# The last nine groups' q and k by rows and DMA transposes in a kernel of chunked attention and a leaky two-layer network

## The chip, the cores and the metric

The kernel runs on one core of a Trainium2 chip. The time is the device's, in microseconds, of one execution; a kernel's time is the median of its runs. The engines are TensorE (PE, with its weight loads PEld), VectorE (DVE), ScalarE (ACT), GpSimd (POOL) and SyncE (SP, which only issues DMAs here). Each engine works off its own instructions in order and waits on semaphores for the others.

## The reference

Inputs are q, k and v of 8 batches, 8 heads, 576 rows and 64 columns, and two weight matrices, all in float32.

```python
q_c = q.reshape(B, H, nc, 64, D)                       # nc = 9 chunks of 64 rows; k_c, v_c alike
scores = scale * np.matmul(q_c, k_c.transpose(0, 1, 2, 4, 3))
scores = scores - np.max(scores, axis=-1, keepdims=True)
attn = np.exp(scores)
attn = attn / (np.sum(attn, axis=-1, keepdims=True) + 1e-09)
out = np.matmul(attn, v_c)                             # attention inside each chunk alone
x = out.transpose(0, 2, 1, 3).reshape(B * S, H * D)    # 4608 tokens of 512
h = x @ w_in                                           # 512 x 2048
g = np.maximum(0.01 * h, h)
return g @ w_out                                       # 2048 x 512, float32
```

## The kernel before

**Attention, 36 groups.** A group u is 128 tokens (two chunks) of all 8 heads. Per group: q goes into a tile QZ (one of three), where each head's q stands transposed beside zeros, so that one matmul does two heads; k goes transposed into KT. Stage s multiplies them into the PSUM bank Sp (8 matmuls, L827). Stage m takes the row maximum on DVE. Then there are two forms: groups in UB (and all before UX = 14) subtract the maximum on DVE (stage b) and take one exponential of 512 columns on ACT (stage x); the others turn the maximum into a bias (stage nb) and take eight exponentials of 64 columns that also give the row sums (stage f). Stage z sums and inverts on DVE, stage n multiplies on POOL (tile en), stage d transposes en by a DMA on SP's queue into et (L916), stage v multiplies by V (L927), and stage a copies the result on ACT into xT, the transposed tokens.

**How q and k come in.** Groups before UD = 14 load their natural rows (load_qk, tiles q_in and k_in, 128 tokens on 128 partitions, cast to 16 bits) by DMAs on POOL's queue, and PE transposes them into PSUM. Groups from 14 on use load_qk_batch: per batch 16 DMAs on POOL's queue (L114) bring q and k in 32 x 32 pieces into the tiles q_d and k_d, and DVE's 32 x 32 transposes finish the work: stage dq writes QZ in two halves of 64 partitions (L804), stage dk writes KT (L814). A group that lies across two batches does each in two pieces. A batch has four and a half groups; batches 3 to 7 come in this way.

**The network, 19 blocks.** Blocks of 128 or 256 tokens follow as soon as their tokens are there. The first layer of a block is mm1 (L347, result hT, leaky unit on ACT at L361) up to block 13; from block 14 on it is done with seven products in place of eight (`wide`, L444, banks xbank and xpr, sums xs and WS of the inputs, kept parts xkeep, leaky unit at L462 on ACT or for the parts in LEAK_DVE at L458 on DVE). The second layer of nearly all blocks is also done with seven products (`product`, L245), from four sums SG of parts of the activations gT (`token_sums`, L221, on DVE) and four sums of weights; `combine` puts the products together (L288 to L309) and the result is stored from SP's queue (L321).

**The order.** PE's work is a list `chunks`, one chunk being some 8 to 16 matmuls. Everything else is an event with a due time in steps; a step is one chunk (half a step for a part of `wide`). A loop issues all events that are due, then the next chunk. The scores of group u are due at T[u], which adds up the distances in SPACE; the other stages of the group are due at fixed distances from T[u] (O_Q for dq and dk, O_Z for z, n and d, O_V and VO for v and a). `later` makes an event some steps after the present chunk, and the dict MOVED shifts single events by name, such as `'dq 32 1': -3.25`. `flush` issues pending events at once where a chunk needs them. So the emitted order on each engine's queue is set by these numbers, and the time by when each queue's head may go.

Of the kernel before, what the change touches and what calls it, by code (L numbers as in the profile page):

```python
# [8 lines left out]
FP16 = mybir.dt.float16  # L9
# [7 lines left out]
def kernel(  # L17
# [22 lines left out]
    NIN = 5  # L40
    PAIRED = range(1, 4)
    UD = 14
    LEAD = 5
    UE = 5
    UX = 14
    UB = (14, 17, 18, 19, 21, 24, 26, 27, 28, 30, 32, 34)
    G = 2 * CH

    NU = n_tok // G
# [159 lines left out]
    def token_sums(j, n):  # L209
        nh = BLOCKS[j] // 2  # L210
        one, two = rows(j)
        a11, a12 = gT[j][:, :HF, one], gT[j][:, HF:, one]
        a21, a22 = gT[j][:, :HF, two], gT[j][:, HF:, two]
        SG[j, n] = sbp.tile([128, HF, nh], FP16, name="SG", tag="gS", bufs=4, padded_shape=[128, HF, 128])
        x, y, op = {
            1: (a21, a22, ALU.add),
            2: (SG.get((j, 1)), a11, ALU.subtract),
            3: (a11, a21, ALU.subtract),
            4: (a12, SG.get((j, 2)), ALU.subtract),
        }[n]  # L220
        nc.vector.tensor_tensor(out=SG[j, n], in0=x, in1=y, op=op)  # L221

    def product(j, n, i):
        one, two = rows(j)
# [584 lines left out]
    def stage_dk(u):  # L809
        KT[u] = sbp.tile([128, 4, 2, CH], FP16, name="KT", tag="KT", bufs=3)  # L810
        for b, at, e0, n in cuts(u):
            for i in range(1, 16, 2):
                need("D", b, i)
            nc.vector.transpose(  # L814
                out=KT[u][:, :, e0:e0 + n, :],
                in_=flat(qkd[b][1])[:, :, at:at + n * CH].rearrange("p h (e t) -> p h e t", e=n),
            )
# [103 lines left out]
    def stage_v(u):  # L921
        et = ET.pop(u)
        xp = psp.tile([128, NT, 2, CH], FP32, name="xp", tag="ox", bufs=1)
        for e in range(2):
            b, c = divmod(2 * u + e, NCH)
            for t in range(NT):
                nc.tensor.matmul(  # L927
                    out=xp[:, t, e, :],
                    lhsT=VB[b % NVB][:, t, c, :],
                    rhs=et[:, t // 2, e, t % 2, :] if u < UD else et[:, t % 2, e, t // 2, :],  # L930
                    start=True,
                    stop=True,
                )
            if c == NCH - 1 and b + NVB < B:
                load_v(b + NVB)
# [48 lines left out]
    def zero_act(i):  # L984
# [162 lines left out]
```

## Time and profile before

| | |
|---|---|
| median of 3 runs | 282.65 us (282.22 to 283.72) |
| profiled execution | 283.47 us, span 281.6 us, granted clock 0.998 |
| PE busy | 271.5 us, 96% of the span |
| PEld busy | 242.1 us, 86% |
| DVE busy | 237.5 us, 84% |
| ACT busy | 189.9 us, 67% |
| POOL busy | 152.5 us, 54% |
| chain that ended last | PE 77%, DVE 9%, DMA 5%, ACT 4% |

A profile row of a group of instructions reads: line, engine, operation, out<-in by tile names, shapes, count, then busy us and mean ns of one, then idle time before them and what ended it. A row of the waits reads: who waited, for whom, us in all, times, longest. A row of the timeline reads: start, duration, engine, line, what, count, and in brackets the idle time before it. A row of stretches gives each engine's busy us and count, the granted clock, the DMA share and GB/s.

### The profile page before, as it was taken

How to read it: one execution, taken by the hardware profiler on the slowest of the kernel's cores; microseconds unless marked ns; L12 is line 12 of the kernel's file. 1: busy time of each engine (PE TensorE's matmuls, PEld its weight loads, DVE VectorE, ACT ScalarE, POOL GpSimd, SP SyncE). 2: the span in 40 equal slices, each digit the busy share in tenths (PEclk: the TensorE clock that was granted, in tenths of full speed). 3: DMA queues.
4: the chain of work that ended last, by engine and by line, in shares of the span. 5: the costliest groups of instructions: out<-in, count | busy, mean ns of one | idle time of the engine just before them, and what ended most of it. 6: DMA issues, size and time to landing. Idle time of an engine off the chain costs nothing.

```text
span 281.6 us, 8496 instructions
## 1 busy us (share of the span) xinstructions
PE 271.5 (96%) x3464; PEld 242.1 (86%) x3464; DVE 237.5 (84%) x471; ACT 189.9 (67%) x485; POOL 152.5 (54%) x182
## 2 busy tenths in 40 slices
PE   7889999999999999999999999999899999999995
PEld 4569958999998888999999999999789898999994
DVE  5876599899887978999978787999999999887674
ACT  6766734675757587657778676567568888786761
POOL 8838636878296687797569828934024151600000
PEclk9999999999999999999999999999999999999999
DMA  9999999999999999999999999999451213110213
GB/s 144 152 190 177 207 175 155 151 120 114 64 100 177 82 60 151 134 165 81 178 81 129 123 249 159 206 100 128 33 95 22 94 21 95 21 74 4 75 40 112
DMA packets 182790, 32.66 MB, mean 116 GB/s; under 512 B 173792, under 2 KB 178272, under 8 KB 182752
## 3 DMA queue, kind: packets, MB, share of 16 engines
q0 software_dynamic: 158880, 18.23, 129.7%
q1 hardware_dynamic: 22832, 13.64, 22.2%
q8 instruction: 27, 0.44, 0.7%
q10 hardware_dynamic: 1040, 0.26, 0.4%
q14 instruction: 11, 0.09, 0.1%
HBM read 36.96 MB, written 9.44 MB: 165 GB/s over the span
## 4 chain that ended last, share of the span: by engine, by line
PE 77%; DVE 9%; DMA 5%; ACT 4%; POOL 2%; issue 2%; DVEq 0%; ACTq 0%; POOLq 0%
PE hT L347 29%; PE prX L245 17%; PE prZ L245 6%; PE pr L245 6%; PE xbank L444 4%; PE xpr L444 3%; DMA VB<-in_v_dram 3%; ACT ex L858 3%; PE prW L245 2%; PE oP L489 2%; DMA k_in<-in_k_dram 2%; PE Sp L827 2%; PE xp L927 2%; DVE xkeep L480 2%; DVE QZ L804 1%
## 5 line engine op out<-in xcount | busy, mean ns | idle before, releaser
L347 PE MATMUL hT<-xT,w_inT 128*128 128x256 f16 (+1 forms) x1088 | 102.9, 248 | 0.6 <-DMA w_inT<-in_moe_w_in_dram 0.6
L347 PEld LDWEIGHTS <-w_inT 128*128 128x128 f16 x1088 | 84.1, 98 | 7.3 <-issue 0.8
L361 ACT ACTIVATE gT<-hT 128x512 f16<-128x512 f32 x104 | 61.8, 606 | 25.7 <-PE hT L347 25.5
L893 POOL TENSOR_TENSOR en<-ex,zi 128x512 f16<-128x512 f16 x26 | 28.6, 1098 | 64.3 <-DVE zi L887 15.3
L245 PEld LDWEIGHTS <-SG 128*128 128x128 f16 x544 | 51.4, 98 | 6.3 <-DVE SG L221 0.7
L245 PEld LDWEIGHTS <-gT 128*128 128x128 f16 x400 | 37.3, 98 | 4.9 <-ACT gT L462 0.8
L114 POOL DMA_DIRECT2D q_d<-in_q_dram x40 | 33.2, 832 | 5.9 <-DVE QZ L804 5.1
L245 PE MATMUL prX<-TW,SG 128*128 128x256 f16 x272 | 35.3, 273 | 0.6 <-DVE SG L221 0.6
L114 POOL DMA_DIRECT2D k_d<-in_k_dram x40 | 32.7, 817 | 1.8 <-DVE KT L814 1.1
L836 DVE TENSOR_REDUCE mx<-Sp 128x8 f32<-128x512 f32 x36 | 24.4, 678 | 9.6 <-PE Sp L827 9.4
L288 ACT ACTIVATE keep<-prX 128x256 f32<-128x256 f32 x51 | 20.1, 394 | 16.8 <-PE prX L245 16.8
L804 DVE STREAM_TRANSPOSE QZ<-q_d 64x512 f16<-64x512 f16 (+1 forms) x48 | 30.9, 650 | 0.6
L858 ACT ACTIVATE ex<-Sp,nb 128x64 f16<-128x64 f32 x80 | 24.0, 331 | 5.3 <-DVE nb L850 5.2
L480 DVE TENSOR_TENSOR xkeep<-xpr,xkeep 128x512 f32<-128x512 f32 x30 | 19.9, 679 | 6.7 <-PE xpr L444 4.4
L941 ACT ACTIVATE xT<-xp 128x512 f16<-128x512 f32 x36 | 21.9, 607 | 5.2 <-PE xp L927 5.2
L221 DVE TENSOR_TENSOR SG<-gT 128x1024 f16<-128x1024 f16 x34 | 23.7, 697 | 1.3 <-ACT gT L361 1.3
L444 PEld LDWEIGHTS <-WS 128*128 128x128 f16 x320 | 19.4, 98 | 1.3 <-issue 0.8
L462 ACT ACTIVATE gT<-xkeep 128x512 f16<-128x512 f32 x25 | 15.6, 632 | 6.7 <-DVE xkeep L480 6.7
L883 DVE TENSOR_REDUCE z<-ex 128x8 f32<-128x512 f16 x26 | 17.5, 672 | 2.7 <-ACT ex L873 2.4
L121 POOL DMA_DIRECT2D VB<-in_v_dram x16 | 18.6, 1169 | 0.4 <-PE xp L927 0.4
L473 ACT ACTIVATE xkeep<-xbank 128x512 f32<-128x512 f32 x30 | 16.7, 600 | 2.3 <-PE xbank L444 2.3
L245 PE MATMUL prX<-w_outT,gT 128*128 128x256 f16 x136 | 17.9, 273 | 0.3 <-ACT gT L462 0.3
(96 smaller groups left out, 470.9 us busy)
## 6 DMA issues: line engine op xcount, KB each, us to landing
out_dram<-osb SPq DMA_DIRECT2D x35, 256.0 KB, 4.4
VB<-in_v_dram POOLq DMA_DIRECT2D x16, 288.0 KB, 7.3
q_d<-in_q_dram POOLq DMA_DIRECT2D x40, 72.0 KB, 5.2
k_d<-in_k_dram POOLq DMA_DIRECT2D x40, 72.0 KB, 5.2
w_inT<-in_moe_w_in_dram POOLq DMA_DIRECT2D x8, 256.0 KB, 7.7
w_outT<-in_moe_w_out_dram POOLq DMA_DIRECT2D x4, 512.0 KB, 11.1
q_in<-in_q_dram POOLq DMA_DIRECT2D x11, 128.0 KB, 8.2
k_in<-in_k_dram POOLq DMA_DIRECT2D x11, 128.0 KB, 7.7
```

What stands on the lines that cost most here:

```text
L114: nc.gpsimd.dma_start(out=t[p0:p0 + 32, m, :, :, :].rearrange("p h b d -> p (h b) d"), in_=src[b, h0:h0 + 2, :, dh * 32:dh * 32 + 32].rear ...
L221: nc.vector.tensor_tensor(out=SG[j, n], in0=x, in1=y, op=op)
L245: nc.tensor.matmul(out=to[:, i, :], lhsT=left[:, f, i * 128:(i + 1) * 128], rhs=right[:, f, :], start=(j, where) not in opened, stop=(f == ...
L347: nc.tensor.matmul(out=hT[:, i, :], lhsT=w_inT[:, t, fc * 128:(fc + 1) * 128], rhs=xT[:, t, r0:r0 + tb], start=(t == 0), stop=(t == NT - 1),)
L361: nc.scalar.activation(out=gT[j][:, nf * a:nf * a + nf, c0:c0 + tb], in_=HT.pop((j, a, p)), func=AFT.Prelu, bias=0.0, scale=1.0, alpha=0.01,)
L444: nc.tensor.matmul(out=to[:, i, :], lhsT=left[:, t, i * 128:(i + 1) * 128], rhs=right[:, t], start=(n in (1, 2, 5) and t == 0 and i == 0), ...
L480: nc.vector.tensor_tensor(out=to, in0=of, in1=to, op=ALU.add)
L804: nc.vector.transpose(out=qz[s * CH:(s + 1) * CH, :, e0:e0 + n, s, :], in_=flat(qkd[b][0])[s * CH:(s + 1) * CH, :, at:at + n * CH].rearran ...
L836: nc.vector.tensor_reduce(out=MX[u], in_=SP[u], axis=AXL.X, op=ALU.max)
L858: nc.scalar.activation(out=E[u][:, i, :], in_=SP[u][:, i, :], func=AFT.Exp, bias=NB[u][:, i:i + 1], scale=SCL, accum_out=Z[u][:, i:i + 1],)
L893: (nc.gpsimd if u >= UP else nc.vector).tensor_tensor(out=E[u], in0=ex, in1=ZI.pop(u).unsqueeze(2).to_broadcast((128, 8, CH)), op=ALU.mult)
L941: nc.scalar.activation(out=xT[:, :, at:at + G], in_=xp, func=AFT.Copy, bias=0.0, scale=1.0)
```

## The change

Groups from UM = 27 on (batches 6 and 7) load natural rows again (load_qk, event g, 12 steps ahead of the transposes). SP's queue then issues two DMA transposes of 128 x 512 each: tdk straight into KT, tdq into a new tile QT, which shares the buffers of q_in. DVE copies the two halves of QT into QZ (stage cq). Stages dq and dk and the batch loads are left for groups 14 to 26 and batches 3 to 5. For these groups the heads stand in natural order again, so stage v takes et as it does before group 14.

Beside this, groups 15 and 25 join UB and group 21 leaves it; the sums 1 and 4 of block 14 move from DVE to POOL (SG_POOL); one part of block 17 moves in the leaky unit from DVE to ACT (LEAK_DVE); five distances in SPACE and nine in VO change, and the events from block 10 on (and the attention stages beside them) get other shifts in MOVED.

```diff
+    UM = 27
-    UB = (14, 17, 18, 19, 21, 24, 26, 27, 28, 30, 32, 34)
+    UB = (14, 15, 17, 18, 19, 24, 25, 26, 27, 28, 30, 32, 34)
...
-        nc.vector.tensor_tensor(out=SG[j, n], in0=x, in1=y, op=op)
+        (nc.gpsimd if (j, n) in SG_POOL else nc.vector).tensor_tensor(out=SG[j, n], in0=x, in1=y, op=op)
...
+    MOVED = {... 'tdq 33': 0.75, 'tdk 33': 1.25, 'cq 32 0': 1.5, 'cq 32 1': 3.5, 'cq 33 0': 2.0, 'cq 34 0': 2.0, 'tdk 34': 2.0, ...}
+    SG_POOL = ((14, 1), (14, 4))
-    LEAK_DVE = ((15, 1, 1, 0), (16, 0, 0, 0), (16, 0, 1, 0), (17, 1, 0, 0), (17, 1, 1, 1))
+    LEAK_DVE = ((15, 1, 1, 0), (16, 0, 0, 0), (16, 0, 1, 0), (17, 1, 0, 0))
-    S_LATER = (0, 1.5, 4, 10.5)
+    S_LATER = (0, 1.5, 4, 12.0)
-    X_LATER = (0.5, 1, 2.5, 4.0)
+    X_LATER = (0.5, 2.5, 2.5, 3.5)
-    D_T = 2.5
+    D_T = 3.0
...
+    def stage_tdk(u):
+        KT[u] = sbp.tile([128, 4, 2, CH], FP16, name="KT", tag="KT", bufs=3)
+        nc.sync.dma_start_transpose(
+            out=KT[u].rearrange("p i e c -> p i (e c)"), in_=qk[u][1].rearrange("p h d -> p (h d)")
+        )
+
+    def stage_tdq(u):
+        QT[u] = sbp.tile([128, 4, 2, CH], FP16, name="QT", tag="q_in", bufs=NIN)
+        nc.sync.dma_start_transpose(
+            out=QT[u].rearrange("p i e c -> p i (e c)"), in_=qk[u][0].rearrange("p h d -> p (h d)")
+        )
+
+    def stage_cq(u, s):
+        made.add(("dq", u, s))
+        part = slice(s * CH, (s + 1) * CH)
+        nc.vector.tensor_copy(out=QZ[u % NQZ][part, :, :, s, :], in_=QT[u][part])
...
-                    rhs=et[:, t // 2, e, t % 2, :] if u < UD else et[:, t % 2, e, t // 2, :],
+                    rhs=et[:, t // 2, e, t % 2, :] if u < UD or u >= UM else et[:, t % 2, e, t // 2, :],
...
+    O_A = 12.0
+    O_B = 15.0
+    O_C = 4.0
...
-        if u >= UD:
+        if u >= UM:
+            at(t - O_A - O_B, "g", u)
+            at(t - O_B, "tdk", u)
+            at(t - O_B + O_R, "tdq", u)
+            at(t - O_C, "cq", u, 0)
+            at(t - O_C, "cq", u, 1)
+        elif u >= UD:
...
-    for b in range(3, B):
+    for b in range(3, -(-UM * G // S)):
```

More of the change, by code (lines that the diff above doesn't have):

```diff
@@ L713, in fill @@
                 later(D_O, "O", j, a)
-    MOVED = {'xs 14 3': 0.5, 'xs 18 1': -2.25, 'xs 16 3': 0.25, 'G 13 6 0': 0.75, 'lp 18 1 0 0': -1.25, 'sum 13 3': -0.25, 'sum 15 4': -2.25, 'lx 16 1 6': -6.75, 'lp 17 1 1 0': 4.0, 'dq 32 1': -3.25, 'combX 13 1': -1.25, 'lp 14 0 0 0': -2.25, 'lp 14 1 0 0': 0.75, 'd 27': 2.25, 'dq 28 0': -5.75, 'sum 13 4': -2.25, 'a 31': 3.0, 'b 34': 1.0, 'lp 14 1 1 1': 0.5, 'lp 14 0 1 1': 2.25, 'lx 15 0 4': 1.0, 'lp 15 1 1 1': 3.5, 'WS 1': -2.5, 'lx 16 0 1': 1.25, 'lx 16 1 7': -1.5, 'sum 13 2': -1.0, 'xs 14 1': -1.25, 'lp 16 0 0 0': 1.0, 'dq 29 1': -2.0, 'combZ 12 3': -6.0, 'lx 14 0 6': 5.75, 'lx 18 1 4': -1.0, 'combW 11 2': 2.25, 'lx 15 0 1': -1.75, 'lx 14 1 1': -2.5, 'WS 4': 3.0, 'f 31 0 4': -0.5, 'lx 16 0 7': -2.25, 'combW 13 2': -0.75, 'lx 16 0 4': -2.75, 'lx 14 1 6': 1.5, 'combX 17 7': -0.75, 'z 35': -0.75, 'sum 15 3': 0.25, 'sum 13 1': -0.25, 'dq 33 0': -1.75, 'a 29': 2.0, 'combW 14 2': -1.0, 'xs 15 1': -2.5, 'combZ 10 3': -0.75, 'z 31': -0.75, 'dq 31 1': 1.75, 'z 30': -0.25, 'xs 16 2': 6.5, 's 30': -1.25, 'm 30': -0.75, 'combZ 13 5': 1.25, 'lx 14 1 7': -1.25, 'xs 14 4': 6.5, 'sum 14 4': 3.5, 'f 29 0 4': -1.25, 'WS 2': -0.25, 'WS 3': 4.25, 'G 13 7 0': 1.75, 'sum 14 1': -0.75, 'xs 15 4': -2.25, 'G 13 3 0': 3.0, 'a 28': 1.0, 'combX 14 6': 1.25, 'lp 15 0 1 1': -0.25, 'dq 31 0': -2.5, 'z 29': -1.5, 'lx 15 0 7': -3.0, 'G 13 1 0': -2.0, 'v 29': -0.5, 'x 34': -0.75, 'combX 13 7': 0.25, 'xs 17 1': 0.25, 'la 17 0 2': 6.0, 'dq 32 0': -0.5, 's 34': -0.5, 'lx 15 1 7': -0.5, 'combZ 14 5': 1.5, 'sum 14 3': -0.75, 'm 34': 0.5, 'dq 35 0': 3.75, 'combX 14 7': 0.25, 'xs 16 1': 0.75, 'd 30': 2.25, 'combX 11 4': 0.25, 'la 15 1 5': 0.5, 'lx 15 1 6': 0.25, 'v 31': -2.25, 'dk 33': -0.5, 'sum 12 1': -2.75, 'G 13 0 0': -1.75, 'xs 16 4': -1.75, 'dq 35 1': -2.75, 'f 27 0 4': -0.25, 'combZ 17 2': 0.5, 'lp 15 0 0 0': -1.25, 'd 31': 4.0, 'G 12 3 0': -1.25, 'combX 12 1': -1.0, 'dq 34 0': -2.25, 'lp 16 0 1 1': -1.75, 'D 7 12': 1.5, 'z 32': -0.75, 'n 29': -1.0, 'sum 17 4': 0.5, 'combX 18 7': -0.75, 'combW 12 2': -1.75, 'dq 29 0': -0.5, 'b 32': 2.0, 'v 26': -0.75, 'G 12 5 0': -2.75, 'sum 11 4': -0.75, 'sum 16 4': -2.75, 'lx 17 1 1': -0.5, 'combX 16 7': 3.75, 'sum 17 2': 0.25, 'lp 14 1 1 0': -3.0, 'xs 18 3': 1.5, 'lx 18 1 7': -2.0, 'combZ 15 3': 3.0, 'd 35': 1.0, 'dq 33 1': 2.0, 'v 33': -0.75, 'sum 11 2': 0.25, 'la 17 1 5': 1.0, 'lx 17 1 4': 3.25, 'combX 14 4': -0.25, 'combX 15 6': -0.25, 'lx 14 0 1': 0.5, 'xs 17 4': 2.0, 'combX 12 6': 0.75, 'xs 18 4': -0.5, 'f 33 4 8': 1.0, 'lp 17 1 0 0': 4.0, 'combX 16 1': -0.25, 'la 18 0 2': -2.0, 'G 12 4 0': 5.0, 'n 30': -0.25, 'la 18 0 5': 2.0, 'lx 14 0 7': -2.5, 'combX 15 4': -0.75, 'la 14 0 3': 0.25, 'sum 12 2': -0.75, 'f 35 4 8': -0.25, 's 33': -0.75, 'sum 17 1': 0.25, 'D 7 8': 0.25, 'sum 16 2': -0.25, 'lx 18 1 1': -0.25, 'lx 17 1 7': 0.25, 'G 11 7 0': 0.25, 'D 7 7': 0.5, 'G 12 2 0': 3.0, 'a 33': -0.25, 'la 17 1 3': -0.5, 'lp 15 1 0 0': -3.0, 'G 12 6 0': 0.25, 'lp 16 0 1 0': 0.75, 'xs 15 2': 5.0, 'la 17 0 3': 1.75, 'dk 34': 0.25, 'D 7 6': -3.0, 'dk 28': 0.5, 'combZ 14 3': -0.75, 'lp 16 1 1 0': -0.75, 'lx 17 1 6': -0.75, 'lx 18 1 6': -0.5, 'v 25': -2.0, 'dq 30 1': -1.0, 'combX 18 1': -0.5, 'v 24': -2.0, 'la 18 1 2': 3.5, 'G 12 0 0': -0.25, 'lp 18 1 1 0': -2.0, 'lx 17 0 6': -0.25, 'f 29 4 8': -0.5, 'sum 14 2': -0.25, 'dk 32': -0.25, 'combX 18 6': -3.0, 'lx 17 0 1': -1.0, 'xs 14 2': 0.75, 'xs 15 3': -0.25, 'v 30': -0.25, 'la 17 1 2': -0.25, 'dq 28 1': -0.75, 'combZ 17 3': 1.0, 'lx 18 0 4': -0.5, 'combZ 18 5': -0.5, 'lx 18 0 1': -0.25, 'combX 15 1': -1.75, 'lp 17 1 1 1': -1.0, 'lx 15 1 1': -0.25, 'G 12 1 0': 0.75, 'a 25': 0.5, 's 28': -2.0, 'd 26': 0.5, 'la 14 0 2': 0.5, 'combZ 11 3': -2.0, 'D 7 13': 0.25, 'combZ 13 3': 0.5, 'dk 31': 3.0, 'lp 16 1 1 1': -0.25, 'combZ 16 5': 2.25, 'combZ 17 5': -0.5, 'la 14 0 5': 0.5, 'combX 15 7': -0.5, 'combX 14 1': -0.5, 'G 13 2 0': -0.75, 'lx 14 0 4': -1.25, 'lx 16 1 1': 0.75, 'lp 16 1 0 0': -0.25, 'combX 11 7': -3.0, 'combZ 18 2': -0.75, 'a 24': -0.5, 'f 33 0 4': 1.0, 'la 16 1 3': -0.25, 'f 31 4 8': -0.25, 'lx 16 1 4': -0.25, 'combX 18 4': 0.25, 'sum 16 1': -0.25, 'combZ 18 3': -0.75, 'xs 17 2': 0.25, 'G 12 7 0': -2.0, 'combW 15 2': -0.25}
@@ L817, in stage_dk @@
             )
+    QT: dict[int, bass.AP] = {}
+    def stage_tdk(u):
[12 more added lines that the diff above has]
+        nc.vector.tensor_copy(out=QZ[u % NQZ][part, :, :, s, :], in_=QT[u][part])
     def stage_s(u):
@@ L1007 @@
         "A": first_layer, "H": first_act, "S": first_sum, "G": act1, "B": second_layer, "O": finish, "i": idle, "y": zero, "w": zero_act,
-        "I": identity, "st": store_held, "nb": stage_nb, "f": stage_f, "dq": stage_dq, "dk": stage_dk, "D": load_qk_batch,
+        "I": identity, "st": store_held, "nb": stage_nb, "f": stage_f, "dq": stage_dq, "tdk": stage_tdk, "tdq": stage_tdq, "cq": stage_cq, "dk": stage_dk, "D": load_qk_batch,
         "WS": w_in_sum, "xs": x_sums, "lx": wide_x, "la": wide_m, "lp": leaky,
@@ L1033 @@
         STAGES[name](*how)
-    SPACE = [4.0, 4.5, 7.0, 5.5, 4.0, 6.0, 6.0, 3.5, 8.5, 7.5, 8.0, 7.5, 5.0, 8.0, 6.5, 5.0, 10.0, 6.5, 8.5, 7.0, 6.5, 10.0, 6.0, 9.5, 5.0, 10.5, 6.5, 9.0, 7.0, 8.0]
-    VO = [-1.5, 1.0, 4.0, 0.0, 1.5, -0.5, 0.5, 1.5, 0.0, 0.5, 4, 1.5, -0.5, 2.5, -0.5, -0.5, -0.5, -2.0, 1.5, 0.0, 3.5, 0.5, -2.0, 1.0, 3.0, 3.5, 0.0, -1.5, -6.0, -2.0]
+    SPACE = [4.0, 4.5, 7.0, 5.5, 4.0, 6.0, 6.0, 3.5, 8.5, 8.0, 7.5, 8.0, 4.5, 8.0, 6.5, 5.0, 10.0, 6.5, 8.5, 7.0, 6.5, 10.0, 6.0, 9.5, 5.0, 10.5, 6.5, 9.0, 8.0, 8.0]
+    VO = [0.5, 1.0, 4.0, 0.0, 0.5, -0.5, 1.5, 0.5, 0.0, 0.5, 4, 1.5, -1.5, 2.5, -0.5, -0.5, -1.5, -2.5, 1.5, 0.0, 3.5, 0.5, -2.0, 1.0, 2.0, 3.5, 0.5, -1.5, -6.0, -2.0]
     O_T = 6
```

1 line of the change is left out of this document (added).

## The prediction

> **What bounds the kernel now.** I read the busy time by stretches first, then what TensorE (PE) waited for, then PE's timeline where it waited.
>
> ```profile
> 60.00:190.00 130.00, 130.00 (x1520) 118.11 (x1518) 113.63 (x228) 88.76 (x245) 91.98 (x105) 1.00 2.26 131
> 190.00:250.00 60.00, 57.54 (x780) 52.53 (x778) 55.96 (x112) 46.30 (x142) 19.09 (x22) 1.00 0.39 64
> 250.00:280.00 30.00, 28.30 (x362) 26.34 (x359) 21.66 (x44) 17.46 (x35) 0.00 (x0) 1.00 0.17 62
> ```
>
> The columns are PE, its weight loads, VectorE (DVE), ScalarE (ACT), GpSimd (POOL), then the granted clock. From 60 to 190 us PE never stops, so nothing done there can gain. From 190 to 250 it does, and DVE has 55.96 of 60 us full. The end of the last stretch is the tail behind the last matmul.
>
> ```profile
> PE Sp L827 <- DVE KT L814: 0.9, 1, 0.9
> PE prX L245 <- DVE SG L221: 0.6, 1, 0.6
> ...
> PE xbank L444 <- ACT xkeep L473: 0.4, 1, 0.4
> ...
> PE prX L245 <- ACT gT L462: 0.3, 1, 0.3
> ...
> PE xpr L444 <- DVE xkeep L480: 0.2, 1, 0.2
> ```
>
> The longest of these waits is for exactly what the change takes off DVE: the scores of a group waited for its K transpose. Together the five are 2.4 us. That is too little, since a matmul's modelled end hides part of a gap; the starts are the better measure:
>
> ```profile
> 200.37 1.04 PE L245 MATMUL prX<-TW,gT 128*128 128x256 f16 x8
> 201.25 1.04 PE L347 MATMUL hT<-xT,w_inT 128*128 128x256 f16 x8
> 203.19 0.66 PE L827 MATMUL Sp<-KT,QZ 128*128 128x64 f16 x8 [0.90 <-DVE KT L814]
> 203.68 1.04 PE L245 MATMUL prZ<-w_outT,SG 128*128 128x256 f16 x8
> 204.55 1.06 PE L444 MATMUL xbank<-xT,w_inT 128*128 128x128 f16 x16
> 205.45 1.04 PE L245 MATMUL prX<-w_outT,gT 128*128 128x256 f16 x8
> ...
> 249.93 0.27 PE L245 MATMUL pr<-w_outT,gT 128*128 128x256 f16 x1
> ```
>
> Undisturbed, eight matmuls of 256 columns start 0.87 us before what follows (203.68 to 204.55), sixteen of 128 columns 0.89 us; eight of 64 columns take 0.23 us in the same list. The 67 rows from 200.37 to 249.93 hold 200, 368 and 96 matmuls of these sizes: 25 x 0.8725 + 23 x 0.893 + 12 x 0.231 = 45.1 us. They took 49.56 us. So PE lost 4.4 us between 200 and 250 us, and that is all that the change can win: PE's own work is unchanged, and the 30 us before the first full stretch and the tail are not touched.
>
> **What comes off DVE.** Groups 27 to 35 lose stages dq and dk. Group 31 straddles two batches and does each in two pieces.
>
> ```profile
> L804 DVE STREAM_TRANSPOSE QZ<-q_d 64x512 f16<-64x512 f16 x40 | 27.9, 697 | 0.5
> ...
> L814 DVE STREAM_TRANSPOSE KT<-k_d 128x512 f16<-128x512 f16 x20 | 14.0, 702 | 0.3
> ...
> L778 DVE COPY QZ<-qp 64x512 f16<-64x512 f16 x20 | 8.7, 433 | 2.5 <-PE qp L751 2.0 <-ACT QZ L776 0.3
> ...
> L885 DVE TENSOR_SCALAR ze<-z 128x8 f32<-128x8 f32 x36 | 6.3, 174 | 3.0 <-ACT ex L858 2.1
> ...
> L412 DVE TENSOR_TENSOR xs<-xT 128x256 f16<-128x256 f16 x4 | 1.1, 282 | 0.0
> ```
>
> Eight whole groups are 16 x 0.697 + 8 x 0.702 = 16.8 us, and group 31 is about one more, 2.1 to 2.5 us: some 19 us. Added are 18 copies (stage cq) of 64x512 in 16 bits, from SBUF to SBUF, which the trace does not have. The same copy out of PSUM takes 433 ns, an upper bound; an instruction on 8 columns takes 174 ns, a lower one. I take 280 ns, the row nearest to them in memory and type (two inputs of 256 columns, 282 ns): 5.0 us, between 3.1 and 7.8. What counts is the part in the stretch where PE waits:
>
> ```profile
> 190.00:215.00 25.00, 5.00 (x9) 0.00 (x0) 1.00 0.68 77
> 215.00:240.00 25.00, 3.48 (x5) 0.00 (x0) 1.00 0.20 60
> ...
> 190.00:215.00 25.00, 2.81 (x5) 0.00 (x0) 1.00 0.68 77
> 215.00:240.00 25.00, 1.44 (x3) 0.00 (x0) 1.00 0.20 60
> ```
>
> The first pair is DVE's work on tile q_d, the second on k_d: 12.7 us of transposes in 50 us, groups 30 to 35. Twelve copies give 3.4 us back (2.1 to 5.2). Net 9.3 us (7.5 to 10.6).
>
> **What else moves on DVE, ACT and POOL.**
>
> ```profile
> L221 DVE TENSOR_TENSOR SG<-gT 128x1024 f16<-128x1024 f16 x34 | 23.7, 697 | 1.3 <-ACT gT L361 1.3
> L893 POOL TENSOR_TENSOR en<-ex,zi 128x512 f16<-128x512 f16 x26 | 28.6, 1098 | 64.3 <-DVE zi L887 15.3 <-ACT gT L361 14.8 <-ACT xkeep L473 11.1
> L412 POOL TENSOR_TENSOR xs<-xT 128x256 f16<-128x256 f16 x6 | 4.7, 786 | 1.2 <-ACT xT L941 1.2
> L114 POOL DMA_DIRECT2D q_d<-in_q_dram x40 | 33.2, 832 | 5.9 <-DVE QZ L804 5.1 <-DMA q_d<-in_q_dram 0.7
> L99 POOL DMA_DIRECT2D q_in<-in_q_dram x15 | 12.2, 820 | 6.7 <-DMA w_outT<-in_moe_w_out_dram 2.5 <-issue 1.5 <-POOLq L1131 0.8
> ```
>
> Sums 1 and 4 of block 14 leave DVE for POOL: 2 x 0.70 = 1.4 us. On POOL, 256 columns cost 0.79 and 512 cost 1.10, so 1024 come to about 1.7 us each if that line is carried on (an estimate). Sum 2 needs sum 1 and product 6 needs sum 2, so this is 1 us more in a chain that runs at the start of block 15; but the sums of block 14 are then first on an idle POOL instead of last on a late DVE, so I count nothing. Without that cover it costs up to the 1 us. Groups 15 and 25 take the form with one exponential and DVE's subtraction and row sum, group 21 leaves it, which is two more 128x512 passes on DVE for each of two groups and two fewer for one; these groups lie in the stretch of full PE, where DVE has 16 of 130 us free: nothing. One part of block 17 leaves DVE for ACT behind 250 us, where ACT has 12 of 30 us free: nothing.
>
> POOL issues 32 loads of batches 6 and 7 less, 32 x 0.83 = 26.6 us, and 20 by rows more (eight groups x 2, group 31 x 4), 20 x 0.82 = 16.4 us. Its work falls by 10 us and gains 3.4 us of sums. It isn't the bound, and the normalized weights it makes are used 8 and mostly 14 steps after they are placed.
>
> **SP's queue and the DMAs.** Eighteen transposes join the 30 that bring the weights et.
>
> ```profile
> L916 SPq DMA_TRANSPOSE et<-en x6: 1192/1201/1465, 206.5 to 242.5; - x6
> ...
> DMA to landing us min/median/max: 2.4/2.4/4.4
> ```
>
> That is the stretch from 200 us on. The tile has the same shape (128 x 512, 16 bits), so one new transpose costs SP 1.2 us and lands 2.4 us after its issue, 4.4 at worst there. Nine pairs are 21.6 us of an SP that mostly waits. tdk stands 15 steps and tdq 13.75 steps before the scores of its group, the copies 4 (single ones are moved, copies by up to 3.5 steps later); a step is one chunk of PE, 0.87 us. So tdq has 9.75 x 0.87 = 8.5 us until the copies, and needs 1.2 + 2.4 to 4.4 = 3.6 to 5.6 us. The load by rows stands 12 steps, 10.4 us, ahead of tdk, and this row gives the like:
>
> ```profile
> q_in<-in_q_dram POOLq DMA_DIRECT2D x11, 128.0 KB, 8.2
> ```
>
> SP is in order: behind a transpose that waits for its load stand the stores of out and the et transposes. Those loads ran in the first 60 us, under the most DMA traffic; the last column but one of the stretches above falls from 2.26 to 0.39 after 190 us, and the loads of batches 6 and 7 in small pieces are gone, so I expect less than 8.2 us and no wait. If SP waited, et would come some us later, and its user (stage v) stands mostly 14 steps behind it.
>
> The Trainium skill speaks against this edit: "VectorE: DVE Perf Modes", section "The three transpose paths", gives 1309 ns for a 128x128 by DMA against 311 ns on VectorE, so four of them would be an estimated 5.2 us, a pair 10.5 us, more than the 8.5 us. The trace does not bear that out: 128 x 512 landed in 2.4 us with its issue.
>
> **The sum.** DVE's load from 190 to 250 us falls from 55.96 by 9.3 + 1.4 to about 45 of 60 us. Three of the five waits name DVE (0.9, 0.6, 0.2), and the wait for ACT's xkeep stands behind exponentials that waited for DVE. What is late next is ACT itself (46.30 of 60 us, with exponentials in rows of eight that hold up gT and xkeep). Of 4.4 us I leave 1.5: the 0.4 and 0.3 with the 0.17 us that each gap costs beside its idle time, and as much again for new places. Gain 2.9 us (bounds: 4.4 if nothing is left, 0 if all stays). The profiled execution took 283.47 us, its span 281.6 and 1.9 around it; 283.47 - 2.9 = 280.6. The median of the runs, 282.65, lies 0.8 lower: 279.8 us. A measurement can tell 0.5% from no change, 1.4 us, so faster ends at 281.2 and slower begins at 284.1.
>
> **Rivals.** *DVE and POOL hold each other up.* In the trace they do:
>
> ```profile
> 241.48 1.53 DVE L221 TENSOR_TENSOR SG<-gT,SG 128x1024 f16<-128x1024 f16 x1
> ...
> 241.14 1.33 POOL L893 TENSOR_TENSOR en<-ex,zi 128x512 f16<-128x512 f16 x1 [5.46 <-ACT gT L462]
> ```
>
> A sum that takes 0.70 took 1.53 while POOL ran: 0.83 us lost. Two sums of 1.7 us on POOL can hold DVE for 3.4 us, and twelve copies that meet POOL's 19.09 of 60 us one time in three lose 4 x 0.83 = 3.3 us. That takes back 6.7 of 10.7 us; with 4/10.7 of the gain left, 1.1 us, the time is 281.6. The Trainium skill has it as a lock ("SBUF — State Buffer", section "Who interferes with whom"): copies in a two-port mode and two-input operations exclude GpSimd for a whole instruction. The row agrees for the two-input case; none shows the copy. Against this rival: POOL has idle stretches of 5 us there.
>
> *SP's queue makes the scores late* (the other side). SP stands still for what is at its head:
>
> ```profile
> SPq L321 <- DVE osb L309: 41.2, 14, 8.4
> ```
>
> A store or et transpose placed ahead of tdq and held for 8.4 us leaves 13.75 x 0.87 - 8.4 = 3.6 us for issue, landing (3.6 to 5.6) and two copies (0.6). From a hold of 7 us on, S waits for cq as it waited for KT. Such a wait cost 203.19 - 201.25 - 0.87 = 1.1 us and 0.2 us of slow start; with 1.3 us at half of the nine groups, 5.9 us less the 2.9 won: 285.6. For it: all loads of q and k now hang on this queue. Against: holds of 7 us are rare, the stores' mean is 41.2/14 = 2.9 us.
>
> *The new places cost more than they give*: most steps from block 10 on are shifted, and 130 to 200 us has no wait to lose but many to get. With one new wait of 1.3 us in each of five blocks, 6.5 - 2.9 is 3.6 us slower; with three, 1.0: 283.7 to 286, 284.5 in the middle.
>
> **How the numbers follow.** Forecast 0.62, port 0.15, SP's queue 0.13, new places 0.10. The forecast's own range is 278.2 (no wait left) to 281.2. The port rival lies in the middle class; the other two are slower. The range reaches from 278.2 to 285.0: it leaves out over half of SP's case, a third of the last and a little below, 0.15 in all.
>
> **What would show it.** Right: no transposes of q_d and k_d after group 26; DVE about 45 of 60 us from 190 to 250; copies near 0.28 us; new transposes landing in 2.4 to 4.4 us; PE's loss there about 1.5 us, with ACT named. Wrong: Sp or the copies waiting for a DMA, DVE's two-input sums stretched beside POOL, or PE waits between 130 and 200 us.

## The result and the profile after

The changed kernel takes 281.4 us (median of 20 runs, 280.2 to 284.1) beside 283.43 us for the kernel before (20 runs, 282.22 to 284.59): ratio 0.9938, interval 0.9918 to 0.9959. It is 0.6% faster. The profiled execution took 281.23 us with a span of 279.5, against 283.47 and 281.6. One of the 12 runs of experiment 4 below and four of the 12 of experiment 7 were in a slower state of the chip, and their numbers leave these runs out.

The stretches of the changed kernel, with the columns as before:

```profile
60.00:190.00 130.00, 130.00 (x1521) 118.44 (x1519) 110.41 (x224) 87.73 (x230) 76.94 (x86) 1.00 1.83 129
190.00:250.00 60.00, 58.44 (x807) 54.13 (x806) 53.17 (x107) 48.26 (x145) 28.16 (x30) 1.00 0.89 112
250.00:280.00 30.00, 26.21 (x334) 24.40 (x332) 18.43 (x39) 16.42 (x34) 0.00 (x0) 0.99 0.15 54
```

PE is still full to 190 us: the new places cost nothing there. From 190 to 250 us it is busier by 0.9 us. DVE fell only from 55.96 to 53.17, not to 45. The DMA share in that stretch rose from 0.39 to 0.89.

What PE waited for, after the first 30 us:

```profile
PE xp L948 <- DMA et<-en: 1.3, 1, 1.3
...
PE Sp L848 <- DVE QZ L838: 0.2, 1, 0.2
```

All five waits of before are gone. Two others stand there, and both are for a DMA transpose: the first names it, the second is a wait for copies that waited for QT. PE's starts in the same stretch as before:

```profile
200.45 1.04 PE L246 MATMUL prX<-TW,gT 128*128 128x256 f16 x8
201.33 1.04 PE L348 MATMUL hT<-xT,w_inT 128*128 128x256 f16 x8
202.57 0.41 PE L848 MATMUL Sp<-KT,QZ 128*128 128x64 f16 x8 [0.21 <-DVE QZ L838]
204.30 0.39 PE L948 MATMUL xp<-et,VB 128*128 128x64 f16 x8 [1.32 <-DMA et<-en]
...
247.84 1.04 PE L246 MATMUL pr<-w_outT,gT 128*128 128x256 f16 x8
```

The same 200, 368 and 96 matmuls took 247.84 - 200.45 = 47.39 us in place of 49.56. Less the 45.12 us of undisturbed work, PE lost 2.3 us in place of 4.4. That is the whole gain: 2.1 us of span. Of the 2.3, 1.5 us is one late et: xp started 1.73 us after the scores before it (202.57 to 204.30), whose eight matmuls of 64 columns take 0.23. Another 0.4 us is the pause before these scores, whose copies waited for a late QT.

SP's queue shows which transposes these were. The first fence is SP's timeline, the others the times from issue to landing of the transposes issued between 190 and 199 us, for et, KT and QT in this order:

```profile
191.40 1.28 SPq L937 DMA_TRANSPOSE et<-en  x1
192.84 1.21 SPq L825 DMA_TRANSPOSE KT<-k_in  x1
194.22 1.39 SPq L831 DMA_TRANSPOSE QT<-q_in  x1
195.71 1.30 SPq L937 DMA_TRANSPOSE et<-en  x1
197.12 1.20 SPq L825 DMA_TRANSPOSE KT<-k_in  x1
201.97 1.19 SPq L831 DMA_TRANSPOSE QT<-q_in  x1
```

```profile
DMA to landing us min/median/max: 4.7/6.6/8.4
...
DMA to landing us min/median/max: 7.9/8.0/8.1
...
DMA to landing us min/median/max: 7.7/7.7/7.7
```

QT issued at 194.22 landed at 201.9, and the copies could start at 201.93. The et issued at 195.71 landed at 204.1, and xp started at 204.30. SP had issued them in time: the multiplication en before that et ran on POOL from 194.63 to 195.67. They were slow on the way. GpSimd's queue (the timeline of POOL) had loads out at that moment, first of all the V of the last batch (VB):

```profile
191.32 2.37 POOL L122 DMA_DIRECT2D VB<-in_v_dram  x2
194.63 1.04 POOL L914 TENSOR_TENSOR en<-ex,zi 128x512 f16<-128x512 f16 x1 [0.95 <-ACT keep L289]
195.62 0.95 POOL L100 DMA_DIRECT2D q_in<-in_q_dram  x1
196.56 0.90 POOL L100 DMA_DIRECT2D k_in<-in_k_dram  x1
```

The kernel before issued the same V load at 190.05 us, with one et transpose beside it and one 5.6 us later, and both landed in good time:

```profile
L916 SPq DMA_TRANSPOSE et<-en x2: 1195/1196/1197, 190.1 to 195.7; - x2
...
DMA to landing us min/median/max: 4.4/4.4/4.5
```

So the V load by itself does not make a transpose slow. In the changed kernel the first et beside it (191.40) landed in 4.7 us too; the four transposes that followed it within 5.7 us, with two loads by rows among them, landed late.

### The profile page after: what moved, and what is told of

Same layout as the page of the kernel before. It is cut to its first block, busy times and chain, and to the rows that moved or that the text cites. A ratio compares the mean times of both kernels' runs of the same rounds, so it can differ in the third digit from the quotient of the medians.

```text
span 279.5 us, 8496 instructions
## 1 busy us (share of the span) xinstructions
PE 270.8 (97%) x3464; PEld 243.0 (87%) x3464; DVE 228.1 (82%) x457; ACT 189.9 (68%) x471; POOL 146.7 (53%) x172
## 4 chain that ended last, share of the span: by engine, by line
PE 82%; DMA 11%; POOL 2%; DVE 2%; ACT 1%; issue 1%; SPq 0%; DVEq 0%; ACTq 0%; POOLq 0%
PE hT L348 28%; PE prX L246 19%; PE xbank L445 6%; PE prZ L246 6%; PE pr L246 6%; PE xpr L445 5%; PE prW L246 3%; DMA VB<-in_v_dram 3%; DMA et<-en 3%; PE xp L948 3%; PE oP L490 2%; PE Sp L848 2%; DMA k_in<-in_k_dram 2%; DMA QT<-q_in 2%; ACT ex L879 1%
## 5 line engine op out<-in xcount | busy, mean ns | idle before, releaser
L100 POOL DMA_DIRECT2D q_in<-in_q_dram x25 | 21.1, 848 | 13.3 <-DMA et<-en 3.6
L100 POOL DMA_DIRECT2D k_in<-in_k_dram x25 | 20.4, 818 | 9.3 <-DMA VB<-in_v_dram 5.5
L879 ACT ACTIVATE ex<-Sp,nb 128x64 f16<-128x64 f32 x72 | 21.6, 327 | 3.8 <-DVE nb L871 3.8
L115 POOL DMA_DIRECT2D q_d<-in_q_dram x24 | 19.9, 829 | 2.1 <-DVE QZ L806 0.8
L904 DVE TENSOR_REDUCE z<-ex 128x8 f32<-128x512 f16 x27 | 18.2, 675 | 2.6 <-ACT ex L894 2.3
L115 POOL DMA_DIRECT2D k_d<-in_k_dram x24 | 19.5, 813 | 0.2 <-DMA q_d<-in_q_dram 0.2
L806 DVE STREAM_TRANSPOSE QZ<-q_d 64x512 f16<-64x512 f16 (+1 forms) x28 | 18.2, 657 | 0.3
```

Of the source, the lines that this page charges most:

```text
L100: nc.gpsimd.dma_start(out=to, in_=rows)
L115: nc.gpsimd.dma_start(out=t[p0:p0 + 32, m, :, :, :].rearrange("p h b d -> p (h b) d"), in_=src[b, h0:h0 + 2, :, dh * 32:dh * 32 + 32].rear ...
L879: nc.scalar.activation(out=E[u][:, i, :], in_=SP[u][:, i, :], func=AFT.Exp, bias=NB[u][:, i:i + 1], scale=SCL, accum_out=Z[u][:, i:i + 1],)
```

## The experiments

The theory: what is left, and what could turn the gain into a loss, is the landing of the transposes beside the load of V of the last batch. Rivals: the order in SP's queue makes them late; the new places are the gain by themselves; one new place of stage v is at fault. All ratios are to the kernel before, measured beside each experiment.

**1. The transposes alone.** The changed kernel with UB, MOVED, LEAK_DVE, S_LATER, X_LATER, D_T, SPACE and VO of before and no sums on POOL:

```diff
-    UB = (14, 15, 17, 18, 19, 24, 25, 26, 27, 28, 30, 32, 34)
+    UB = (14, 17, 18, 19, 21, 24, 26, 27, 28, 30, 32, 34)
...
-    SG_POOL = ((14, 1), (14, 4))
+    SG_POOL = ()
...
```

> The loads by rows, the DMA transposes and the copies of groups 27 to 35 alone, with all old places, groups in UB and sums on VectorE. Theory (VectorE's relief is the gain): the wait of the scores for KT goes, the waits for VectorE's sums and xkeep shrink, PE's loss between 200 and 250 us falls from 4.4 to about 2.5 us, 281.5 us beside a kernel before of 283.4. Rival (the new places are the gain, the transposes only move waits): within 0.5 us of the kernel before, with waits for DMA landings in the place of those for VectorE.

Measured 284.31 us, ratio 1.0023 (0.9991 to 1.0056): no gain. The theory of pure relief missed; the rival's time and its DMA wait were right, though not its premise that the new places are the gain (experiment 2). PE's waits and DVE's timeline of this kernel:

```profile
PE Sp L848 <- DVE QZ L838: 2.6, 1, 2.6
```

```profile
204.80 0.59 DVE L838 COPY QZ<-QT 64x512 f16<-64x512 f16 x2 [2.27 <-DMA QT<-q_in]
```

DVE stood idle for 2.27 us with the copies of group 31 at its head, because QT, issued at 195.6 us, took 9.2 us to land. DVE's work had gone, and a DMA's landing had taken its place.

**2. The places alone.**

```diff
-    UM = 27
+    UM = 36
```

> The changed kernel with UM = 36: all new places, SG_POOL, UB and LEAK_DVE, but groups 27 to 35 loaded by batch and transposed by VectorE as before. Theory (relief is the gain): no faster than the kernel before, 283.4 us or up to 2 us slower, since the old stages dq and dk lack their tuned places. Rival (places are the gain): 281.5 us.

Measured 284.57 us, ratio 1.0040 (1.0015 to 1.0064), with a wait of 2.1 us of the scores for KT on DVE. The rival is out: without the relief the new places cost 0.4%. With the V load where it is, the gain of the change needs both together; experiment 11 shows that this hangs on the V load.

**3. The sums back on DVE.**

```diff
-    SG_POOL = ((14, 1), (14, 4))
+    SG_POOL = ()
```

> The changed kernel with sums 1 and 4 of block 14 back on VectorE. On GpSimd they took 2.13 and 2.17 us and a small VectorE instruction beside the first took 1.29 us in place of 0.17. Theory (VectorE has room from 215 us on): within 0.3 us of the changed kernel, since PE lost under 0.3 us between 215 and 250 us in it. Rival (the two sums were needed off VectorE): 0.7 us or more slower than the changed kernel, with PE waiting for SG near 224 us.

Measured 282.31 us, ratio 0.9956 (0.9934 to 0.9978). The interval overlaps that of the changed kernel, so the time doesn't decide. No wait for SG appeared; PE waited for copies instead (1.3 us in three waits, against 0.2), one of them 0.59 us at 226 us, where the changed kernel has none. This is a sign that the two sums are better off DVE, and no more.

**4. Stage v of group 29 later.**

```diff
-    'v 29': -5.25
+    'v 29': -2.0
```

> The changed kernel with stage v of group 29 placed 3.25 steps later (shift -2.0 in place of -5.25), about 2.8 us. In the changed kernel PE waited there 1.3 us for et, whose transpose took 8.4 us to land. Theory (that one landing is the main part of what is left): the wait at 204 us goes, 1.3 to 1.5 us faster than the changed kernel, 279.9 beside 281.4. Rival (another wait lies right behind it): the wait goes but PE then waits for xs, gT or SG of blocks 13 and 14, less than 0.5 us gained.

Measured 282.12 us, ratio 0.9943 (0.9912 to 0.9973). The wait for et went, as both expected, and the time stayed within noise: the rival was right, though not in what came next. PE now waited 0.41 and 0.84 us for copies of groups 31 and 32, 0.46 us for xkeep. So the place of stage v let that one late et hurt, but moving it alone gains nothing that the runs can show.

**5. No load of V for the last batch** (two DMAs of 288 KB):

```diff
-            if c == NCH - 1 and b + NVB < B:
+            if c == NCH - 1 and b + NVB < B - 1:
```

> The changed kernel without the load of V of batch 7 (two DMAs of 288 KB issued at 191 to 194 us); groups 31 to 35 then multiply by the V of batch 5, so the values of that last batch are left out. Theory (the transposes land late because they share the DMA engines with the loads from GpSimd's queue, the V load above all): the four transposes issued at 192 to 198 us land in under 6 us in place of 7.7 to 8.4, PE's waits for et and QZ near 202 us go, PE's loss falls from 2.3 to under 1 us, 1.3 us or more faster than the changed kernel. Rival (the transposes hold each other up in SP's queue, order is the cause): landings stay at 7 us or more and the time within 0.4 us of the changed kernel.

Measured 280.63 us, ratio 0.9897 (0.9875 to 0.9919). Landings from 190 to 199 us, et, KT and QT:

```profile
DMA to landing us min/median/max: 4.0/5.0/6.0
...
DMA to landing us min/median/max: 4.0/4.6/5.1
...
DMA to landing us min/median/max: 3.1/3.8/4.6
```

SP issued the same five transposes in the same order (a sixth followed at 198.84), and the five landed in 4.0 to 6.0 us in place of 4.7 to 8.4. So the V load is a cause of the late landings in this kernel, and the order in SP's queue alone is not. That the two meet in the shared DMA engines is the theory's reading; no run separates it from another way in which they could meet. The 0.4% over the changed kernel come to 1.2 us. PE's loss didn't fall under 1 us, though: 1.0 us stayed before the scores of group 32.

**6. The same load, later.** Nothing is left out; the load of batch 7 becomes an event nine steps on:

```diff
-            if c == NCH - 1 and b + NVB < B:
+            if c == NCH - 1 and b + NVB == B - 1:
+                later(9, "vl", b + NVB)
+            elif c == NCH - 1 and b + NVB < B:
                 load_v(b + NVB)
```

> The changed kernel with the load of V of batch 7 issued 9 steps, about 8 us, later. Theory (shared DMA engines): the transposes issued at 192 to 198 us land in 5 to 6 us, and those of group 32 and et of group 30 (202 to 207 us) become the slow ones, with 6 to 8 us; the first have users at 202 us, the second some 9 us behind them, so PE's loss falls to 1 us and the time by 1 us. Rival (a wait only moves): the same time as the changed kernel, with PE waiting for the copies of group 32 at 212 us.

Measured 280.29 us, ratio 0.9898 (0.9867 to 0.9928), as fast as without the load. It beats the kernel before clearly; against the changed kernel the intervals overlap a little (0.9918 to 0.9928), but three kernels with that load out of the way lie at 0.990, and the profile (279.48 us, span 277.7) agrees. The load was issued at 195.9 in place of 191.3 us, 4.6 us later and not 8: POOL ran it as soon as it stood at the head of its queue, right behind the loads by rows at 194.10 and 195.04. What the edit changed is the order in POOL's queue. Landings from 190 to 199 us:

```profile
DMA to landing us min/median/max: 3.7/4.2/4.8
...
DMA to landing us min/median/max: 2.7/3.9/5.0
...
DMA to landing us min/median/max: 4.0/5.4/6.8
```

The late transposes that were expected for group 32 did not come: none issued from 199 to 209 us took over 5.6 us.

**7. Transposes three steps earlier.**

```diff
-    O_B = 15.0
+    O_B = 18.0
```

> The changed kernel with loads by rows and transposes of groups 27 to 35 three steps, about 2.6 us, earlier (O_B = 18). Theory: the copies no longer wait (0.4 and 0.2 us of PE gained at 202 and 212 us), the wait for et at 204 us stays, since its transpose still runs beside the V load: 0.3 to 0.6 us faster than the changed kernel. Rival (order in SP's queue): the new transposes now stand further ahead of the et transposes and hold these up, 0.5 us or more slower.

Measured 284.89 us (mean of eight runs, their median 285.18), ratio 1.0042 (1.0006 to 1.0079): the theory's gain missed, the rival was right in sign. Its PE timeline:

```profile
202.23 0.59 PE L948 MATMUL xp<-et,VB 128*128 128x64 f16 x8 [3.27 <-DMA et<-en]
202.63 3.26 PE L348 MATMUL hT<-xT,w_inT 128*128 128x256 f16 x16
205.73 1.04 PE L246 MATMUL prX<-TW,gT 128*128 128x256 f16 x8
```

The loads by rows moved with the transposes, and POOL issued six loads between 190 and 198 us (two of V, four by rows) in place of four; the et transposes took 9.9 and 8.2 us. The order in SP's queue had a part too, as the rival said: the first of them was ready at 190.16, when en ended, and went out at 192.32, behind a QT (190.38) and a store (191.65). So some 2 us of its delay are order, and the rest is a landing of 9.9 us where the changed kernel has 4.7.

**8. One pair of loads later.**

```diff
+    'g 33': 4.0
```

> The changed kernel with the loads by rows of group 33 (two DMAs of 128 KB at 195.6 and 196.6 us) 4 steps, 3.5 us, later. Theory (shared DMA engines): they leave the time in which et of group 29 lands, which falls from 8.4 us by 1 to 3 us; 0.5 to 1.3 us faster. Rival (the V load alone is at fault): landing and time within 0.3 us of the changed kernel.

Measured 281.43 us, ratio 0.9928 (0.9903 to 0.9954). But the edit did not move the loads:

```profile
L100 POOL DMA_DIRECT2D q_in<-in_q_dram x1: 946/946/946, 195.5 to 195.5; - x1
```

The changed kernel issued this load at 195.62, also right behind en. The order in POOL's queue had stayed the same, and POOL does not wait for the steps. So this is in effect the changed kernel once more (its transposes of 192 to 198 us took 8.3 to 8.9 us), and it decides nothing: whether the loads by rows add to the late landings stays open. Experiment 1 hints that they do. It had two more of them, at 198.22 and 199.09, and its four transposes issued from 194 to 199 us took 9.2 to 11.0 us.

**9. Best so far, with the copies of group 32 earlier.** Experiment 6, and:

```diff
-    'cq 32 0': 1.5, 'cq 32 1': 3.5
+    'cq 32 0': -1.0, 'cq 32 1': -1.0
```

> The kernel with the later V load, and the two copies of group 32 placed at shift -1.0 in place of 1.5 and 3.5. In the kernel with the later V load alone PE lost 1.0 us before the scores of group 32, where the two copies took 1.80 us beside GpSimd's loads and sums in place of 0.59. Theory (the copies were placed too late for a VectorE held up by GpSimd): they run near 205.5 us, where VectorE was idle for 0.78 us, the wait goes, PE's loss from 180 us on falls from 1.4 to 0.5 us, 0.8 to 1.0 us faster than with the later V load alone. Rival (group 32's transposes are the limit): the copies then wait for QT and hold up the sums of block 13 behind them; no gain or a loss.

Measured 280.21 us, ratio 0.9898 (0.9865 to 0.9932). The wait before those scores went, no pause of PE over 0.3 us is left after 30 us, and the span is 277.3 beside 277.7. But the runs can't tell it from experiment 6; the expected 0.8 us is not shown.

**10. The kernel before with the later V load** (the edit of experiment 6 alone).

> The kernel before with the same later V load. Theory (the V load harms only through the new transposes): within 0.5 us of the kernel before, whose waits from 200 us on are for VectorE and ScalarE. Rival (the later V load is a gain of its own): 2 us faster, as in the changed kernel.

Measured 283.29 beside 283.30 us, ratio 1.0007 (0.9988 to 1.0026). With q and k of the last groups transposed on DVE, the V load's place is worth nothing.

**11. Experiment 1 with the later V load.**

> The transposes alone on the old places, with the later V load. With the V load at its old place PE waited 2.64 us there for the copies of group 31, whose transpose took 9.2 us to land. Theory (the V load turned the relief into that wait): landing 5 us, the wait goes, 281 us beside 283.5 for the kernel before, so the transposes alone gain too. Rival (the old places are at fault): the wait stays above 1.5 us, or another of that size takes its place; no faster than the kernel before.

Measured 281.26 us, ratio 0.9938 (0.9912 to 0.9963), against 1.0023 (0.9991 to 1.0056) with the V load where it was. QT landed in 4.1 us:

```profile
DMA to landing us min/median/max: 4.1/4.1/4.1
```

and the waits left after 30 us are these:

```profile
PE xp L948 <- DMA et<-en: 0.8, 2, 0.5
PE xbank L445 <- ACT xkeep L474: 0.5, 1, 0.5
```

The theory held. The transposes alone, on the old places, are worth what the whole change brought, once one load of 576 KB no longer goes out ahead of them. Moving the V load does nothing for the kernel before; by the ratios it is worth 1.1 us for the changed kernel (0.9938 to 0.9898) and 2.4 us for the transposes alone (1.0023 to 0.9938). The second difference is clear of the noise, the first only nearly.

## Why the prediction was right or wrong

**Right: the bound.** PE lost 4.4 us from 200 to 250 us and nothing from 60 to 190, and that was the ceiling. The best kernel here is 1.0% faster, its span 4.3 us shorter, with 0.7 us of loss left from 180 us on; nothing went beyond.

**Right: the waits for DVE go.** All three of them, and both for ACT too, are gone. The 1.5 us that I left were put on ACT and on new places; the rest lies with late transposes.

**Wrong: the landing of the transposes.** The step "one new transpose costs SP 1.2 us and lands 2.4 us after its issue, 4.4 at worst there" failed. SP's 1.2 us was right (1.19 to 1.39 in most rows). The landing was 7.7 to 8.4 us for the four transposes issued from 192.84 to 197.12 us. I took it from the stretch after 200 us in the kernel before, which has no loads, while the change issues loads by rows up to 210 us and sets more transposes into the time of the last V load. No et of the kernel before took 8 us: its 30 landed in 2.4 to 7.2 us, median 4.9, and the two beside that V load in 4.4 and 4.5. These two rows with experiments 5 and 6 show what was missing: the V load together with the change's own traffic, the other transposes and perhaps the loads by rows. With 8 us the step's own margin (8.5 us, 3.6 to 5.6 needed) is gone.

**Wrong: the margin of et.** The wait that cost most was for an et transpose, which the kernel before has too. The prediction left it out, since "its user (stage v) stands mostly 14 steps behind it". In groups 27 to 35 of the changed kernel O_V, VO and MOVED leave 8 to 14.25 steps, and for group 29 only 9.75, where the kernel before has 14.5. At 0.87 us a step that is 8.5 us, room enough for a landing of 4.4 us behind en, but not for one of 8.4.

The two steps together cost 0.8 us: 2.3 us lost in place of 1.5, a gain of 2.1 in place of 2.9. That it was no more is luck in part. The 1.5 us left in the sum stood for waits for ACT and for new places; ACT's waits all went, and late landings took up 1.9 us.

**Wrong: the base.** I took the 0.8 us between the profiled execution and the median of three runs as given and subtracted it. Over 20 runs the median before is 283.43, almost the profiled execution's 283.47. So 279.8 should have been 280.6 by its own sum; the measured 281.4 is 1.6 us above the forecast, half from each of the two errors.

**DVE's load** fell by 2.8 us, not by 10.7. DVE's transposes are gone and two sums moved, but the twelve copies took 6.4 us in place of 3.4:

```profile
L838 DVE COPY QZ<-QT 64x512 f16<-64x512 f16 x12 | 6.4, 533 | 0.4 <-DMA QT<-q_in 0.2
...
L871 DVE TENSOR_SCALAR nb<-mx 128x8 f32<-128x8 f32 x4 | 2.4, 588 | 0.1
```

A copy by itself takes 0.23 to 0.29 us, so the 0.28 was the right price without company. Beside POOL it took up to 1.06 us, over the 0.43 that I had as upper end, and four small nb took 2.4 us in place of 1.1. PE's faster run also brings some 2 us of later work into the stretch (an estimate: the rows of xkeep and osb are 0.8 us longer each, and there are 17 sums as before, though two moved to POOL). The port rival had the mechanism and nearly the price: the copies took 3.0 us more, it said 3.3. The row for the copies is there now: 0.23 us alone, 0.96 while en ran on POOL (194.86 on DVE, 194.63 on POOL). With this row the trace agrees with the Trainium skill's lock ("SBUF — State Buffer", section "Who interferes with whom") for the copies too. In the changed kernel the slow copies cost PE only the 0.2 us before 212.66. In experiments 5 and 6, where the late et is gone, PE waited 0.8 us for the copies of group 32, which took 1.8 us in place of 0.6, so there they are the next limit.

**SP's queue as the other side** was the right place, but the cause was the time on the way and not a store held at the head. Experiment 1 is the nearest to that rival: the scores waited 2.6 us for copies whose QT was late, 284.3 us against the forecast 285.6. In experiment 7, 284.9 us, it is an et that is late, in part by its place in the queue. SP's head did stand in the changed kernel for 3.6 us, from 198.32 to 201.97, until an earlier QT had landed, but no user was waiting for what stood behind it.

The other reason against the edit was an estimated 5.2 us for a 128x512 by DMA, from the Trainium skill ("VectorE: DVE Perf Modes", section "The three transpose paths"). I put it aside by the 2.4 us. The rows differ from it both ways, 2.4 us with little traffic and 8.4 beside the V load and the change's own traffic; no single price holds.

**New places from 130 to 200 us** brought no wait; the one that hurt, stage v of group 29, stands at 204 us. One slip of arithmetic in that rival: the middle of 283.7 to 286 is 284.9, not 284.5. Nothing hangs on it.

## What to carry to other kernels

Do not price a DMA by its landing in a quiet stretch, and not by a stretch with only a part of the traffic that the change will make: the same transpose took 2.4 us alone, 4.4 beside the V load, and 7.7 to 8.4 beside the V load with other transposes and loads by rows close by. When work moves from an engine to DMAs, list what else is in flight at the deadline, also for the transfers that were there before, and work out each user's margin from its own place and not from the usual one. Try to move a large load out of the way: here a change of order that delayed one load by 4.6 us was worth some 1.1 us, beside 2.0 for the change itself. When you shift an event, look in the trace whether it moved: a shift acts through the order in a queue, and one that changes no order changes nothing (experiment 8). And measure the base with as many runs as the forecast's size needs.

## What the runs showed of the hardware

PE's granted clock fell after a pause in the middle of full work, but not every time. After 3.27 us of waiting (experiment 7) the next sixteen matmuls took 3.10 us in place of 1.75, at a clock of 0.57 from 202 to 206 us; after 2.09 us (experiment 2) the clock was 0.59 for 4 us. After 2.64 us (the profiled execution of experiment 1) it stayed at 1.00. So the length of the pause alone doesn't decide, and a pause of 2 us can cost 1.6 us more than itself.

```profile
202.00:206.00 4.00, 3.77 (x27) 2.91 (x27) 1.35 (x5) 1.16 (x3) 2.33 (x3) 0.57 1.99 149
```

```profile
205.00:209.00 4.00, 3.91 (x41) 3.36 (x40) 2.52 (x7) 2.42 (x17) 0.69 (x1) 0.59 0.40 121
```

The first is a stretch of experiment 7, the second of experiment 2, with PE first and the clock third from the end.

The mean clock of each run tells the same. One stretch of 4 us at 0.58 lowers the mean over 281 us by 0.006 (worked out from these two rows). Of the twelve runs of experiment 1, six have a mean clock of 0.987 to 0.994 and took 284.6 to 286.2 us; the six at 0.998 or above took 282.1 to 284.0, in the mean 283.1, which is no real gain over the kernel before either (283.6). In the changed kernel six of 20 runs are at 0.987 to 0.994, with a median of 282.6 us against 281.1 for the rest. In the kernel before, whose longest wait of PE after 30 us is 0.9 us, it is 3 of 76 runs. So a late landing seems to cost the median twice, by the wait and in some runs by the clock behind it.

Why transposes land so late when the V load meets the other transposes and the loads by rows is open, and so is the share of each. The V load comes as two DMAs of 288 KB; one of half the size wasn't tried, nor the transposes further apart.
